# Attention with a feed-forward network on one core: all sixteen blocks of the network in one kind of sweep

## The chip, the core and the metric

The kernel runs on one core of a Trainium2 chip. The core has TensorE (matmuls, PE in the profile), VectorE (DVE), ScalarE (ACT), GpSimd (POOL) and SyncE (SP), which issues most DMA transfers. The metric is the device time of one execution in microseconds (us). A profile's own span leaves out what lies around the execution, here 1.7 us.

## The reference

Attention over 4 batches of 8 heads, 1152 keys of 64 dimensions, with queries pooled in pairs to 576; then a feed-forward network on 2304 tokens of width 512, with 2048 hidden units and a slope of its own for each negative hidden value. The weights are float64 and reach the kernel as pairs of 32-bit words.

```python
def _attn_ref(q, k, v) -> np.ndarray:
    B, H, S, D = q.shape
    factor = 2
    scale = 1.0 / np.sqrt(D)
    q_pool = q.reshape(B, H, S // factor, factor, D).mean(axis=3)
    scores = scale * np.matmul(q_pool, k.transpose(0, 1, 3, 2))
    scores = scores - np.max(scores, axis=-1, keepdims=True)
    attn = np.exp(scores)
    attn = attn / (np.sum(attn, axis=-1, keepdims=True) + 1e-09)
    return np.matmul(attn, v).astype(np.float32)
...
def _moe_ref(x, w_in, w_out, alpha) -> np.ndarray:
    h = x @ w_in
    g = np.maximum(h, 0.0) + alpha * np.minimum(h, 0.0)
    return (g @ w_out).astype(np.float32)
```

## The kernel before, in words

**A planner writes the order.** The kernel adds tasks (`Scheduler.add`), each with an engine, an assumed duration, what it reads and writes and a priority. `Scheduler.run` places them one by one at the earliest time by its own clock; among the tasks of an engine that could start within a slack, the lowest priority number goes first, and `NUDGE` shifts the numbers of single tasks. The order so found is each engine's program order; the durations play no part on the chip. Tasks marked `lock` (VectorE's operations that read two tiles of SBUF and GpSimd's additions) are placed one at a time. `Ring` is a set of buffers of one size, `Banks` a set of PSUM banks.

**Attention.** The 32 heads go in 16 pairs (n = 0, 2, ...). A pair's two heads stand on the two halves of the partitions; its 576 queries go in two halves of 288 (half number n + h). Per pair, `pair_prep` loads q and k and splits them into a high and a low part, `pair_max` computes the row maxima (24 matmuls of 384 columns at L851 and four short pairs at L858, each reduced by VectorE at L872). `half_main` does nine chunks per half: eight matmuls of scores (L987), two exponentials on ScalarE (L1004) into one of the slots `pa`, sums of the exponentials over chunks on GpSimd and VectorE (L1017; per half five on GpSimd, two on VectorE), and, once a half, a block of 36 matmuls of the exponentials with V (L1031). `pair_end` adds up the sums with matmuls (L1055), then normalises: the sums go through memory, VectorE and ScalarE make a high and a low part of the result (L1094, L1101, L1106), stored as `xs` (L1114).

**Feed-forward.** The hidden units form 16 blocks of 128. `mm3` (L497) is three matmuls (high by high, high by low, low by high). `hidden` (L507) makes one block for one range of tokens: four `mm3` over the width, two ReLUs on ScalarE (L525, L530), their combination on VectorE (L535), a rounded copy on ScalarE (L541) and the remainder on VectorE (L546). Four more `mm3` per block add to the four output tiles. Blocks 0 to 4 go first, in `low_sweep` (L553): eight ranges of 288 tokens; the partial outputs are copied by ScalarE (L573) and stored to `yp` (L577). Then `high_sweep` (L581) takes blocks 5 to 15 over five ranges of 464 or 460 tokens, loads the partial outputs (L598), adds them on VectorE (L622) and stores the result (L631).

**Weights.** Each block has two halves (first and second layer) of 512 KB. `w_convert` (L418) loads one (L423), takes the size on ScalarE (L426) and makes the value in four VectorE operations (L429, L435, L441, L447); `w_split` rounds it on ScalarE (L407) and takes the remainder on VectorE (L410). There are two buffers for each intermediate. The ten of blocks 0 to 4 run during attention, their place among the pairs set by `W0` to `W3`; six (blocks 5 to 7) go into the buffers of k once the last maxima are there (`maxed[RM]`); the other 16 go to a pool that opens where attention's pool is closed (L1221).

**Banks.** `share` (L1144) divides eight PSUM banks among scores, maxima and hidden units: `EARLY` at first, `LATE` once half `SWITCH` is placed. In `LATE` the hidden units may use banks 1 to 6, so feed-forward matmuls may be placed before attention is over.

Of the kernel before, what the change touches and what calls it, by code (L numbers as in the profile page):

```python
# [10 lines left out]
F32 = mybir.dt.float32  # L11
F32R = mybir.dt.float32r
# [14 lines left out]
ENTER, LEAVE = 160, 135  # L27
# [77 lines left out]
class Task:  # L105
    __slots__ = ("eng", "dur", "emit", "deps", "takes", "prio", "col", "left", "next", "end", "avail", "size", "kind", "dma", "lock", "fixed")


class Scheduler:
# [62 lines left out]
    def run(self, done):  # L172
        while not done():
            best = None
            for eng in range(5):
                at, pick, key = None, None, None
                cand = []
                for t in self.ready[eng]:
                    s = self.start_of(t)
                    if s is not None:  # L180
                        s = max(s, self.free[eng])
                        if eng == PE and self.col and not t.col:
                            s += self.turn
                        cand.append((s, t))
                if not cand:
                    continue
                at = min(c[0] for c in cand)
                for s, t in cand:
                    if s <= at + self.slack[eng]:
                        p = t.prio + (self.col_cost if eng == PE and t.col != self.col else 0.0)  # L190
                        if key is None or p < key:
                            key, pick, first = p, t, s
                if eng == PE and self.col and not pick.col:
                    first -= self.turn
                if best is None or first < best[0]:
                    best = (first, pick)
            assert best is not None, "nothing can run"
            self.place(*best)

    def place(self, at, t):  # L200
# [20 lines left out]
        if t.dma:  # L221
            self.dma_free = max(self.dma_free, t.end + 650) + t.size / DMA_RATE
# [11 lines left out]
def attention_ffn(  # L234
# [8 lines left out]
    NLO: int = 5,  # L243
    PB: int = 13,
# [4 lines left out]
    F0: float = -1.353,  # L249
    F2: float = -1.339,  # L250
# [7 lines left out]
    TO_PE: int = 80,  # L258
    FROM_PE: int = 40,
    SLP: int = 39,  # L260
    SLA: int = 62,
    SLD: int = 104,
    QL: float = -0.025,
    KL: float = 0.788,
    KR: float = 2.427,
    KS: float = 0.177,
    M0: float = 1.185,
    E0: float = 1.24,
# [4 lines left out]
    SR: float = 0.765,  # L273
    KQ: float = 0.979,
# [3 lines left out]
    SF: int = 16,  # L278
    Q0: float = 0.075,
    Q1: float = 3.179,  # L280
# [8 lines left out]
    GSB: int = 1,  # L289
    YSB: int = 4,  # L290
    R0: float = 4.187,
    R1: float = -5.36,
    R2: float = -7.727,
    R3: float = -0.231,
    W0: float = 6.13,
    W1: float = 0.815,
    W2: float = 17.603,
    W3: float = -1.085,
    YL: float = 0.25,
    MS: float = 0.129,  # L300
# [3 lines left out]
    GL: float = 16.906,  # L304
    COL: float = -0.047,
    HW: float = 2.585,
    XB: int = 4,
    PT: int = 17,
# [8 lines left out]
    RP: float = 28.496,  # L317
    RS: float = 0.985,
    RM: int = 30,
    RATE: float = 342.662,  # L320
    NP: float = 19.419,
# [148 lines left out]
    for r in (r_x, r_pos, r_neg, r_gs, r_ys):  # L470
        r.open(fpool)
# [804 lines left out]
```

## Time and profile before

| | us |
|---|---|
| time, median of three runs (lowest, highest) | 828.28 (827.81, 828.72) |
| time of the profiled execution | 828.34 |
| its span | 826.6 |
| TensorE busy | 818.3 |
| VectorE busy | 545.3 |
| ScalarE busy | 441.0 |
| GpSimd busy | 252.8 |

Matmuls overlap in the profile, and a busy time counts an operation from its start to its end, waits inside it included. The chain is found backwards from the last instruction: at each step to what released it, or to the instruction before it on its engine. A row such as `41.25 4.51 PE bank L1031 x36` is a piece of that chain: start, length, engine, what is written, line, number of instructions.

### The profile page before, as it was taken

How to read it: one execution, taken by the hardware profiler on the slowest of the kernel's cores; microseconds unless marked ns; L12 is line 12 of the kernel's file. 1: busy time of each engine (PE TensorE's matmuls, PEld its weight loads, DVE VectorE, ACT ScalarE, POOL GpSimd, SP SyncE). 2: the span in 40 equal slices, each digit the busy share in tenths (PEclk: the TensorE clock that was granted, in tenths of full speed). 3: DMA queues.
4: the chain of work that ended last, by engine and by line, in shares of the span. 5: the costliest groups of instructions: out<-in, count | busy, mean ns of one | idle time of the engine just before them, and what ended most of it. 6: DMA issues, size and time to landing. Idle time of an engine off the chain costs nothing.

```text
span 826.6 us, 17555 instructions
## 1 busy us (share of the span) xinstructions
PE 818.3 (99%) x6694; PEld 690.1 (83%) x6694; DVE 545.3 (66%) x1035; ACT 441.0 (53%) x1124; POOL 252.8 (31%) x196
## 2 busy tenths in 40 slices
PE   8999999999999999999999999999999999999997
PEld 7777777777787777777789999998898988888986
DVE  8999999999997798788853888822242332332422
ACT  4757676677675676666744667643243243322431
POOL 5755466465566565565360000000000000000000
PEclk9999999999999999999999999999999999999999
DMA  7335335644444443213233867780330411030301
GB/s 266 74 88 177 111 93 156 221 150 125 99 116 132 120 127 117 63 51 103 93 123 113 263 227 229 207 235 8 92 93 2 136 47 46 1 91 0 92 1 46
DMA packets 67904, 93.72 MB, mean 113 GB/s; under 512 B 20020, under 2 KB 45676, under 8 KB 67820
## 3 DMA queue, kind: packets, MB, share of 16 engines
q1 hardware_dynamic: 65084, 87.71, 34.0%
q0 software_dynamic: 2160, 4.42, 3.6%
q8 instruction: 52, 0.85, 0.4%
q10 hardware_dynamic: 576, 0.47, 0.2%
q14 instruction: 32, 0.26, 0.1%
HBM read 73.48 MB, written 19.02 MB: 112 GB/s over the span
## 4 chain that ended last, share of the span: by engine, by line
PE 96%; DVE 1%; DMA 1%; POOL 1%; issue 0%; ACT 0%; DVEq 0%
PE bank L499 49%; PE bank L987 20%; PE bank L1031 17%; PE bank L851 6%; PE bank L1055 2%; PE bank L858 1%; DMA qs<-qt 1%; DVE bx L872 1%; PE bank L1169 1%; POOL k L814 0%; POOL pa L1017 0%; DVE pa L1017 0%; PE bank L889 0%; DVE wbits L435 0%; POOL qs L773 0%
## 5 line engine op out<-in xcount | busy, mean ns | idle before, releaser
L1017 POOL TENSOR_TENSOR pa<-pa,pa 128x576 f32<-128x576 f32 x160 | 231.2, 1468 | 169.5 <-ACT pa L1004 32.1
L872 DVE TENSOR_REDUCE bx<-bank 128x1 f32<-128x384 f32 (+1 forms) x448 | 212.8, 534 | 24.2 <-PE bank L851 19.0
L1004 ACT ACTIVATE pa<-bank 128x288 f32<-128x288 f32 x576 | 198.8, 417 | 28.1 <-PE bank L987 16.5
L987 PE MATMUL bank<-q,k 64*128 64x288 f32 x1728 | 204.4, 311 | 0.1
L987 PEld LDWEIGHTS bank<-q,k 64*128 64x128 f32 x1728 | 159.5, 184 | 17.4 <-issue 7.2
L1031 PE MATMUL bank<-pa,vv 128*64 128x288 f32 x1152 | 146.8, 409 | 0.0
L1031 PEld LDWEIGHTS bank<-pa,vv 128*64 128x64 f32 x1152 | 79.9, 137 | 54.8 <-issue 3.7
L987 PE MATMUL bank<-mq,neg 64*128 64x288 f32 x576 | 112.5, 291 | 0.0
L851 PE MATMUL bank<-k,q 64*128 64x384 f32 x384 | 107.8, 361 | 1.7 <-ACT q L703 1.3
L535 DVE SCALAR_TENSOR_TENSOR gs<-gs,nal 128x460 f32<-128x460 f32 (+1 forms) x55 | 38.4, 698 | 92.4 <-ACT gs L530 92.4
L499 PE MATMUL bank<-wlow,wh 128*128 128x460 f32 (+1 forms) x320 | 92.9, 371 | 0.0
L499 PE MATMUL bank<-gw,wh 128*128 128x460 f32 (+1 forms) x320 | 92.8, 371 | 0.0
L546 DVE TENSOR_TENSOR gw<-gs,gw 128x460 fp32r<-128x460 f32 (+1 forms) x55 | 35.1, 639 | 85.2 <-ACT gw L541 85.2
L541 ACT ACTIVATE gw<-gs 128x460 fp32r<-128x460 f32 (+1 forms) x55 | 32.4, 589 | 92.9 <-PE bank L499 83.7
L987 PEld LDWEIGHTS bank<-mq,neg 64*128 64x128 f32 x576 | 80.5, 184 | 0.0
L525 ACT ACTIVATE gs<-bank 128x460 f32<-128x460 f32 (+1 forms) x55 | 30.6, 557 | 88.2 <-PE bank L499 87.2
L851 PEld LDWEIGHTS bank<-k,q 64*128 64x128 f32 x384 | 61.3, 184 | 14.0 <-DVE bx L872 5.6
L499 PEld LDWEIGHTS bank<-wlow,wh 128*128 128x128 f32 x320 | 60.1, 188 | 7.1
L499 PEld LDWEIGHTS bank<-gw,wh 128*128 128x128 f32 x320 | 60.1, 188 | 6.7
L499 PE MATMUL bank<-x,wlow 128*128 128x288 f32 x480 | 65.6, 295 | 0.0
L499 PE MATMUL bank<-gs,wlow 128*128 128x288 f32 x480 | 64.8, 294 | 0.0
L499 PEld LDWEIGHTS bank<-x,wlow 128*128 128x128 f32 x480 | 64.1, 188 | 0.8 <-issue 0.8
(90 smaller groups left out, 1022.9 us busy)
## 6 DMA issues: line engine op xcount, KB each, us to landing
wraw<-wt SPq DMA_DIRECT2D x32, 512.0 KB
vv<-vt SPq DMA_DIRECT2D x32, 288.0 KB
xs<-x SPq DMA_DIRECT2D x32, 288.0 KB
x<-xs SPq DMA_DIRECT2D x32, 288.0 KB
kk<-kt SPq DMA_DIRECT2D x15, 576.0 KB
r<-rrd SPq DMA_DIRECT2D x64, 72.0 KB
yp<-ys SPq DMA_DIRECT2D x32, 144.0 KB
wlow<-xs SPq DMA_DIRECT2D x16, 288.0 KB
```

What stands on the lines that cost most here:

```text
L499: nc.tensor.matmul(out=ps[:, :n], lhsT=w[a, c // DMO][:, c % DMO:c % DMO + P], rhs=lo(hl), start=(first and i == 0), stop=(last and i == 2),)
L525: ACT, act(n, True), lambda: nc.scalar.activation(out=flat(pos), in_=ps.t[:, :n], func=AF.Relu),
L535: lambda: nc.vector.scalar_tensor_tensor(out=flat(pos), in0=flat(neg), scalar=nal[:, f:f + 1], in1=flat(pos), op0=ALU.mult, op1=ALU.add),
L541: ACT, act(n), lambda: nc.scalar.activation(out=gs.t[:, 0, :n], in_=flat(pos), func=AF.Copy),
L546: lambda: nc.vector.tensor_tensor(out=gs.t[:, 1, :n], in0=flat(pos), in1=gs.t[:, 0, :n].bitcast(F32), op=ALU.subtract),
L851: nc.tensor.matmul(out=ms.t[:, :JW], lhsT=w.q1.t[d, starts[t]:starts[t] + P], rhs=w.k1.t[d, j * JW:(j + 1) * JW], start=True, stop=True,)
L872: nc.vector.tensor_reduce(out=bx.t[:, at, j:j + 1], in_=ms.t[:, :m], axis=AX.X, op=ALU.max)
L987: nc.tensor.matmul(out=ps.t[i][:, :HQ], lhsT=k.t[d, s] if k else neg[d], rhs=r.t[d, q], start=x == 0, stop=x == len(pairs) - 1,)
L1004: lambda ps=ps, p=p, i=i: nc.scalar.activation(out=p.t[:, i], in_=ps.t[i][:, :HQ], func=AF.Exp, scale=SCALE),
L1017: lambda a=a, b=p, part=part, e=e: e.tensor_tensor(out=part.t, in0=a.t, in1=b.t, op=ALU.add),
L1031: nc.tensor.matmul(out=av.t[i * D:(i + 1) * D, :HQ], lhsT=w.vv[i].t[:, e], rhs=p.t[:, i], start=(e == 0), stop=(e == NC - 1),)
L1055: nc.tensor.matmul(out=ps.t[g * 32:(g + 1) * 32, :HQ], lhsT=ones, rhs=acc[n + g // 2][j].t[:, g % 2], start=j == 0, stop=j == m - 1, tile_ ...
```

## The change

The division into low and high sweeps is gone, and with it the partial outputs. `sweep` takes one range of 464 or 460 tokens through all 16 blocks and copies the four output tiles from PSUM once. The x tiles are as wide as a range and have six buffers; those of the first range are loaded during attention (`RX`), those of the next while the current one runs. Hidden units have no bank in `EARLY` or `LATE`: they get banks when all of attention's matmuls are placed. The buffers of the normalisation move to a pool of their own, so the pool for the last 16 weight halves opens without waiting for it. The ten early conversions are one evenly spaced list (`W0` + `W1` c); the six late ones go by `RP` + `RS` c with a negative step. In the last range the last `YT` blocks' output matmuls go tile by tile. The planner's costs for changing the array's tiling are other, `SWITCH` moves from 13 to 29, slots for exponentials from 13 to 18, and all numbers of the plan, `NUDGE` among them, are new (cut here).

```diff
--- before.py
+++ after.py
-ENTER, LEAVE = 160, 135
+ENTER, LEAVE, QUARTER, NARROW = 160, 135, 135, 330
...
+def mode(col):
+    return min(col, 2)
+
+
+def change(a, b):
+    if mode(a) == mode(b):
+        return 0
+    if b > 1:
+        return NARROW
+    return (ENTER if b else LEAVE) + (QUARTER if a == 3 else 0)
...
-            if t.col != self.col:
-                dur += ENTER if t.col else LEAVE
+            dur += change(self.col, t.col)
...
-    NLO: int = 5,
-    PB: int = 13,
+    NE: int = 10,
+    PB: int = 18,
...
-    W0: float = 6.13,
-    W1: float = 0.815,
-    W2: float = 17.603,
-    W3: float = -1.085,
-    YL: float = 0.25,
+    R0: float = -2.0,
+    W0: float = 8.38,
+    W1: float = 2.392,
+    YL: float = 0.15,
...
-    LATE: tuple = ((0, 1, 2, 3, 4, 5, 6), (0, 1, 2, 3, 4, 5, 6), (1, 2, 3, 4, 5, 6)),
-    SWITCH: int = 13,
+    LATE: tuple = ((0, 1, 2, 3, 4, 5, 6), (0, 1, 2, 3, 4, 5, 6), ()),
+    SWITCH: int = 29,
...
-    HW: float = 2.585,
-    XB: int = 4,
-    PT: int = 17,
+    HW: float = -13.26,
+    XB: int = 6,
+    RX: float = 35.673,
+    PT: int = 18,
...
-    RP: float = 28.496,
-    RS: float = 0.985,
+    RP: float = 64.684,
+    RS: float = -1.529,
...
+    YT: int = 3,
...
-    r_x = Ring([P, 2, HQ], F32R, "x", XB)
-    r_low = Ring([P, 2, DMO], F32R, "wlow", 2 * NLO)
+    r_x = Ring([P, 2, max(NW)], F32R, "x", XB)
+    r_low = Ring([P, 2, DMO], F32R, "wlow", NE)
...
-    r_pos = Ring([P, HQ], F32, "pos", 3)
-    r_neg = Ring([P, HQ], F32, "neg", 2)
-    r_gs = Ring([P, 2, HQ], F32R, "gs", NLO + GSB)
-    r_ys = Ring([P, HQ], F32, "ys", YSB)
...
+    r_gs = Ring([P, max(NW)], F32, "gs", GSB)
+    r_ys = Ring([P, max(NW)], F32, "ys", YSB)
...
-    yp = [[dt(f"yp{b}_{j}", [P, KD, HQ], F32) for j in range(2)] for b in range(B)]
-    yp_b = [[Buf() for j in range(2)] for b in range(B)]
...
-    def low_sweep(b, j, prio):
...
-    def high_sweep(first, n, prio, end):
...
-        x, ys = [Buf(r_low) for k in range(KD)], [Buf(r_x) for m in range(KD)]
+    def x_load(first, n, prio, deps=()):
         row("z", first)
+        x = [Buf(r_x) for k in range(KD)]
...
+    def sweep(x, first, n, prio, end):
+        row("z", first)
+        ys = [Buf(r_ys) for m in range(KD)]
+        fs = range(NFF)
+
+        def tail(f, m, p):
+            return prio + 0.05 * (fs[-1] - fs[0]) + YL + 0.001 * m if end and f > NFF - 1 - YT else p
+
         y = [Buf(r_y) for m in range(KD)]
         prev = [None] * KD
-        fs = range(NLO, NFF)
         for f in fs:
-            p = prio + 0.05 * (f - NLO)
-            gs = hidden(f, x, n, p, True)
+            p = prio + 0.05 * f
+            gs = hidden(f, x, n, p)
...
                 t = add(
                     DVE, dve(hi - lo),
-                    lambda m=m, lo=lo, hi=hi: nc.vector.tensor_tensor(
-                        out=flat_of(ys[m], F32)[:, lo:hi], in0=y[m].t[:, lo:hi], in1=flat_of(ys[m], F32)[:, lo:hi], op=ALU.add
-                    ),
-                    deps=[prev[m]] + ys[m].writers[:len(list(parts(first, n)))], uses=[y[m], ys[m]], prio=prio,
+                    lambda m=m, lo=lo, hi=hi: nc.vector.tensor_copy(out=ys[m].t[:, lo:hi], in_=y[m].t[:, lo:hi]),
+                    reads=[y[m]], writes=[ys[m]], deps=[prev[m]], prio=prio,
                 )
...
+        bp = ctx.enter_context(tc.tile_pool(name="norm", bufs=1))
         ap = actx.enter_context(tc.tile_pool(name="attn", bufs=1))
...
-        for r in (r_vv, r_qs, r_q1, r_q2, r_mm, r_avs, r_rs, r_rc, r_r, r_x2):
+        for r in (r_vv, r_qs, r_q1, r_q2, r_mm):
             r.open(ap)
+        for r in (r_avs, r_rs, r_rc, r_r, r_x2):
+            r.open(bp)
...
-        for i in range(2):
-            for f in range(NLO):
-                r = int(R2 + R3 * f if i else R0 + R1 * f)
-                w_convert(f, i, W2 + W3 * f if i else W0 + W1 * f, [maxed[max(0, r)]], r_low, first=loads[LW:LW + 1] if LW >= 0 else ())
+        for c in range(NE):
+            r = max(0, int(W0 + W1 * c + R0))
+            w_convert(c // 2, c % 2, W0 + W1 * c, [maxed[r]], r_low, first=loads[LW:LW + 1] if LW >= 0 else ())
         rings = [r for r in (r_kk, r_k1, r_k2) for i in range(2)]
         for c in range(REUSE):
-            f, i = NLO + c // 2, c % 2
+            f, i = (NE + c) // 2, (NE + c) % 2
             w_convert(f, i, RP + RS * c, [maxed[RM]], rings[c], loads[-2:])
-        for b in range(B):
-            for j in range(2):
-                low_sweep(b, j, FF + 2 * b + j)
+        x = x_load(0, NW[0], RX, [maxed[RM]])
...
-        attn = [u for r in (r_ps, r_av, r_ms, r_one) for b in r.made for u in b.users]
+        attn = [
+            u for r in (r_ps, r_av, r_ms, r_one, r_vv, r_qs, r_q1, r_q2, r_mx, r_rt, r_mq, r_bx, r_mm, r_p, r_acc)
+            for b in r.made for u in b.users
+        ]
...
-            w_convert(f, i, 2 * FF + 0.05 * (f - NLO) - HW)
+            w_convert(f, i, 2 * FF + 0.05 * f - HW)
     for i, n in enumerate(NW):
-        high_sweep(sum(NW[:i]), n, 2 * FF + i, i == len(NW) - 1)
+        if i:
+            x = x_load(sum(NW[:i]), n, 2 * FF + i - 1)
+        sweep(x, sum(NW[:i]), n, 2 * FF + i, i == len(NW) - 1)
```

## Rows read from the trace of the kernel before

**Rows 1.** The page, chain that ended last: shares of the span by engine.

```profile
PE 96%; DVE 1%; DMA 1%; POOL 1%; issue 0%; ACT 0%; DVEq 0%
```

**Rows 2.** The chain in order of time, whole span: start us, us, what.

```profile
41.25 4.51 PE bank L1031 x36
...
133.59 4.52 PE bank L1031 x36
...
196.22 4.52 PE bank L1031 x36
...
246.79 4.51 PE bank L1031 x36
...
382.11 4.52 PE bank L1031 x36
...
399.61 1.78 PE bank L499 x12
...
413.57 6.57 PE bank L499 x48
...
424.65 9.64 PE bank L499 x72
434.30 1.11 PE bank L1055 x16
435.40 385.87 PE bank L499 x2148
```

**Rows 3.** Busy us by stretch and engine (instructions), clock, DMA share, GB/s.

```profile
core 0: us, PE busy (x) PEld busy (x) DVE busy (x) ACT busy (x) POOL busy (x), PEclk, DMA share, GB/s
50.00:100.00 50.00, 49.96 (x524) 37.71 (x522) 47.04 (x98) 33.53 (x93) 29.27 (x21) 1.00 0.36 110
200.00:250.00 50.00, 50.00 (x541) 38.62 (x537) 46.97 (x96) 35.48 (x98) 29.83 (x22) 1.00 0.48 135
250.00:300.00 50.00, 50.00 (x537) 37.46 (x537) 40.51 (x82) 32.83 (x93) 29.87 (x22) 1.00 0.40 115
350.00:382.00 32.00, 32.00 (x365) 25.14 (x357) 27.52 (x54) 20.86 (x61) 19.76 (x14) 1.00 0.21 67
382.00:434.00 52.00, 52.00 (x495) 41.90 (x492) 39.25 (x58) 32.81 (x93) 25.56 (x16) 1.00 0.34 108
455.00:535.00 80.00, 80.00 (x606) 80.00 (x605) 68.31 (x132) 53.20 (x130) 0.00 (x0) 1.00 0.74 230
```

**Rows 4.** The chain in 436 to 545 us and in 545 to 822 us.

```profile
436.00 109.11 PE bank L499 x824
...
544.97 276.30 PE bank L499 x1322
```

**Rows 5.** VectorE in order of time, 430 to 436 us: the last sum.

```profile
432.90 0.76 DVE L1017 TENSOR_TENSOR pa<-pa,pa 128x576 f32<-128x576 f32 x1 [2.99 <-POOL pa L1017]
```

**Rows 6.** Groups of VectorE, 382 to 434 us: xcount, busy us, mean ns.

```profile
L546 DVE TENSOR_TENSOR gs<-pos,gs 128x288 fp32r<-128x288 f32 x5 | 5.1, 1035 | 1.0 <-ACT gs L541 0.9
```

**Rows 7.** Groups of the whole span, shapes apart: feed-forward and conversions on VectorE.

```profile
L546 DVE TENSOR_TENSOR gs<-pos,gs 128x288 fp32r<-128x288 f32 x40 | 21.0, 526 | 7.3 <-ACT gs L541 7.2
L535 DVE SCALAR_TENSOR_TENSOR pos<-neg,nal,pos 128x288 f32<-128x288 f32 x40 | 20.5, 514 | 10.4 <-ACT neg L530 9.1
L429 DVE TENSOR_SCALAR wbits<-wraw 128x512 int32<-128x512 int32 x32 | 15.8, 493 | 1.1 <-DMA wraw<-wt 1.1
L435 DVE SCALAR_TENSOR_TENSOR wbits<-wraw,wbits 128x512 int32<-128x512 int32 x32 | 21.8, 682 | 0.2
L441 DVE SCALAR_TENSOR_TENSOR wbits<-wraw,wbits 128x512 int32<-128x512 int32 x32 | 23.0, 721 | 0.3
L447 DVE SCALAR_TENSOR_TENSOR wmag<-wmag,wbits 128x512 f32<-128x512 f32 x32 | 22.7, 708 | 0.3
L410 DVE TENSOR_TENSOR wl<-wmag,wh 128x512 fp32r<-128x512 f32 x16 | 10.9, 688 | 3.7 <-ACT wh L407 3.5
```

**Rows 8.** Instructions of the last 16 weight halves' tile: ns min/median/max, first, last.

```profile
L410 DVE TENSOR_TENSOR wl<-wmag,wh x16: 680/691/693, 464.2 to 533.1; 128x512 fp32r<-128x512 f32 x16
```

**Rows 9.** The chain in 812 to 827 us: after the last matmul.

```profile
821.30 0.40 DVE x L622
```

More of the change, by code (lines that the diff above doesn't have):

```diff
@@ L221, in place @@
         if t.dma:
-            self.dma_free = max(self.dma_free, t.end + 650) + t.size / DMA_RATE
+            self.dma_free = max(self.dma_free, t.end + 650) + t.size / (DMA_RATE * (0.8 if at < 20000 else 1))
             t.end = self.dma_free
@@ L474, in attention_ffn @@
     xs_b = [Buf() for b in range(B)]
-    yp = [[dt(f"yp{b}_{j}", [P, KD, HQ], F32) for j in range(2)] for b in range(B)]
-    yp_b = [[Buf() for j in range(2)] for b in range(B)]
-    def x_load(b, j, prio):
-        xk = [Buf(r_x) for k in range(KD)]
-        for k, x in enumerate(xk):
-            add(
-                SP, 600, lambda k=k, x=x: nc.sync.dma_start(out=x.t.bitcast(F32), in_=xs[b][k, j]),
-                reads=[xs_b[b]], writes=[x], prio=prio + 0.0001 * k, size=P * 2 * HQ * 4,
-            )
-        return xk
     def parts(first, n):
@@ L505, in mm3_time, with hidden @@
         return 3 * (n * 17 / 16 / 2.4 + 4.5)
-    def hidden(f, x, n, prio, wide):
-        ps, pos, neg, gs = Buf(r_h), Buf(r_gs if wide else r_pos), Buf(r_gs if wide else r_neg), Buf(r_gw if wide else r_gs)
+    last_hidden = []
+    def hidden(f, x, n, prio):
+        ps, pos, neg, gs = Buf(r_h), Buf(r_gs), Buf(r_gs), Buf(r_gw)
         def flat(buf):
@@ L514, in hidden, with mm @@
         t = None
-        step = 1 if wide else KD
-        for lo in range(0, KD, step):
-            def mm(lo=lo):
-                for kd in range(lo, lo + step):
-                    mm3(ps.t, n, f, kd * P, lambda hl: x[kd].t[:, hl, :n], kd == 0, kd == KD - 1)
-            t = add(PE, step * mm3_time(n), mm, reads=x[lo:lo + step] + [w_done[f, 0]], writes=[ps],
-                    deps=[t] if t else [], prio=prio, kind="group" if lo else "first")
+        for kd in range(KD):
+            def mm(kd=kd):
+                mm3(ps.t, n, f, kd * P, lambda hl: x[kd].t[:, hl, :n], kd == 0, kd == KD - 1)
+            t = add(PE, mm3_time(n), mm, reads=[x[kd], w_done[f, 0]], writes=[ps], deps=[t] if t else last_hidden[-1:], prio=prio, kind="group" if kd else "first")
+        last_hidden.append(t)
         add(
@@ L631, in high_sweep @@
                         lambda m=m, b=b, j=j, q=q, c=c, lo=lo, e=e: e.dma_start(
[L632 removed]
+                            out=out[b, j, m, :, q], in_=ys[m].t[:, lo + c.start:lo + c.stop]
                         ),
@@ L1064, in pair_end @@
         e = n + E0
-        add(PE, 486 * len(acc[n]), sums, reads=acc[n] + acc[n + 1], writes=[ps], prio=e, col=2, kind="s")
+        add(PE, 486 * len(acc[n]), sums, reads=acc[n] + acc[n + 1], writes=[ps], prio=e, col=3, kind="s")
         add(
@@ L1215, in attention_ffn @@
         r_h.places = [single[i] for i in (0, 1, 2, 7)]
-        attn = [
-            u for r in (*(() if REUSE else (r_kk, r_k1, r_k2)), r_vv, r_qs, r_q1, r_q2, r_mx, r_rt, r_mq, r_bx, r_mm, r_p, r_acc, r_avs, r_rs, r_rc, r_r, r_x2)
-            for b in r.made for u in b.users
-        ]
-        sch.run(lambda: all(t.end is not None for t in attn))
     hpool[0] = ctx.enter_context(tc.tile_pool(name="hpool", bufs=1))
-    r_gw.open(hpool[0])
-    for f in range(NLO, NFF):
+    for r in (r_gw, r_gs, r_ys):
+        r.open(hpool[0])
+    for f in range(NFF):
         for i in range(2):
```

101 lines of the change are left out of this document (33 added, 68 removed).

## Prediction

> **What bounds the kernel now.** I read the chain that ended last first, then the same chain in order of time, then the busy time of each engine by stretch, and last the rows of the operations that share a stretch with the change. The chain is TensorE for 96% of the span [rows 1]: what does not stand on TensorE's lane costs nothing until it makes that lane wait. In order of time the lane has two parts [rows 2]. Up to 435.40 us it carries attention: each half of a pair of heads ends in one block of 36 matmuls of weights times V, and these blocks mark the pace. From 435.40 us one unbroken run of 2148 feed-forward matmuls takes 385.87 us. Before that, three pieces of feed-forward matmuls (12, 48 and 72) fill 1.78 + 6.57 + 9.64 = 17.99 us of the attention's last 36 us. So the feed-forward work takes 17.99 + 385.87 = 403.86 us of the lane, and attention without it would end at 435.40 - 17.99 = 417.41 us.
>
> The second bound shows in the stretches [rows 3]. VectorE is busy 47.0 us of every 50 up to 250 us (94%), while ten of the weight conversions run, and 40.51 + 27.52 of 82 us (83%) after them. The pace of the halves follows it [rows 2]: half 1 to 8 (41.25 to 133.59) 13.19 us a half, 8 to 17 (to 246.79) 12.58, 17 to 28 (to 382.11) 12.30.
>
> All terms below are differences to the profiled execution: span 826.6 us, time 828.34 us, 0.06 us above the median of the runs, 828.28.
>
> **Feed-forward matmuls.** Before: 8 x 24 x 5 = 960 of 288 columns and 5 x 24 x 11 = 1320 of 464 or 460. After: 5 x 24 x 16 = 1920 of the wide kind, with the same mix of 464 and 460. On the lane the narrow ones take 109.11/824 = 0.1324 us and the wide ones 276.30/1322 = 0.2090 us [rows 4]. After: 1920 x 0.2090 = 401.28 us, against 403.86: **-2.6 us**, the change of the array's tiling at the edges of the three pieces included. Per column that is little, since (0.2090 - 0.1324)/172 = 0.445 ns a column leaves only 4 ns per matmul that do not depend on columns.
>
> The Trainium skill (TensorEngine Tiling (Array Packing), Instruction Overhead) gives each matmul about 60 cycles of overhead. Read as a cost added to each, at 2.4 GHz, the 360 matmuls that vanish would be worth an estimated 9 us and the time would be about 6.4 us below my forecast; the slope between the two sizes above speaks against that reading, and the sum goes by the rows.
>
> **Partial outputs.** 32 evictions on ScalarE, 32 stores and 48 loads on SP's queue go away, and 21 adds on VectorE become copies of the same size. All of it lay under the unbroken run of TensorE [rows 2, 4]: **0**. Without that cover it would be worth something only at the seam near 545 us, where the lane shows no gap.
>
> **Ten early conversions.** They move from 45 to 240 us to positions 2.4 halves apart, from half 8 on, none before the maxima of half 6. VectorE's load evens out to (200 x 0.94 + 132 x 0.83)/332 = 0.896. On the line between the two paces (12.58 at 0.94, 12.30 at 0.83) that is 12.47 us a half; 27 halves from 41.25 to 382.11 take 336.7 us, not 340.9: **-4.2 us**. Bounds: 0, if only the place of the delay moves, and 27 x 12.30 = 332.1, which is -8.8. The other new numbers of the plan (18 slots for exponentials, not 13; start-up priorities; other costs for the array's changes) I cannot price from rows: 0, with 2 us either way.
>
> **The end of attention.** No bank is given to hidden units until every attention matmul is placed, so on TensorE's queue the first feed-forward matmul now stands behind the last sums, and all feed-forward work behind it. The 17.99 us of filler are gone: does the lane wait instead? Before, the last partial sum ends at 432.90 + 0.76 = 433.66 us [rows 5], the sums start 0.64 us later and take 1.11 [rows 2]. From 382 to 434 us VectorE is busy 39.25 and GpSimd 25.56 of 52 us, together more than the stretch holds [rows 3], since the planner and the chip let VectorE's two-input operations and GpSimd's additions go one at a time: VectorE's residual subtract takes 1035 ns there [rows 6] and 526 over the whole run [rows 7]. So these two engines, not TensorE, end the attention. Taking away the five feed-forward pairs of operations there gives 5 x (0.514 + 0.526) = 5.2 us [rows 7]: last sum at 428.5, end of attention at 430.2, or 430.2 - 417.4 = 12.8 us of idle lane, if all six late conversions stay ahead of the last addition as before. Each that falls behind it gives 0.493 + 0.682 + 0.721 + 0.708 + 0.688 = 3.29 us back [rows 7]. The six are now taken in reverse order: the two that need a place of the low part of K come first, and must wait for the scores of half 29 and half 31, each holding one of two intermediate buffers, so that mostly one conversion circulates, not two. I take three ahead and three behind: 12.8 - 9.9 = **+2.9 us**. Bounds: 0 (two ahead; the lane then has its own work) and 12.8.
>
> The Trainium skill (SBUF — State Buffer, SBUF: two separate sides) says that a VectorE operation with two SBUF inputs and a GpSimd operation take a shared pair of ports as an exclusive lock, and the loser waits for the whole instruction. By that rule the work of both simply adds up, which is the second case below at its worst; did they share the ports, the additions would run beside the conversions, the wait would be 0 and the time 821.0. The 1035 ns agree with the rule.
>
> **Weights of blocks 8 to 15.** They have 16 conversions, which had 133 us of narrow sweeps and now lie in the first wide sweep of 80 us. A block takes 24 x 0.2090 = 5.0 us, so block 15 is due 75 us into the sweep. Before, the same 16 ended 464.2 to 533.1 us [rows 8], 68.9/15 = 4.6 us each, with VectorE at 68.31 of 80 us [rows 3]. The room opens with the end of attention, since the normalising buffers have moved out of it; the first ends some 3 us after that, the 15th at 3 + 14 x 4.6 = 67 us, 8 before it is due: **0**. Between sweeps, six x buffers mean that two of four tiles of the next sweep wait for the last hidden block; 36 output matmuls x 0.2090 = 7.5 us cover their loads. Bounds 0 and some 6 us for both.
>
> **The end.** The last three blocks' outputs are regrouped, so that three of four output tiles end earlier than the 0.63 us apart of before; after the lane's end there still stand one half-tile copy of 0.40 us [rows 9] and its store. **-0.5 us**, bounds 0 and -1.
>
> Sum: -2.6 - 4.2 + 2.9 - 0.5 = -4.4; 828.3 - 4.4 = **823.9 us**.
>
> **The rivals.**
> - Slower, by the port. All six conversions stay ahead of the last addition: 828.3 - 2.6 - 4.2 + 12.8 - 0.5 = 833.8 us. It turns into a loss when the wait passes 2.6 + 4.2 + 0.5 = 7.3 us, that is with the fifth conversion ahead. For it: the fullness of 382 to 434 us. Against: the reversed order, and more slots for sums.
> - Starved sweeps. The conversions need over 5.2 us each, or the x loads outlast their 7.5 us: +6 us, 830 us. For it: VectorE's 85%. Against: the 8 us to spare.
> - It does not do what it says for attention: the pace after half 17 came from the wider sharing of PSUM banks, which now begins at half 29, not 13. No gain of 4.2, and 11 x 0.28 = 3.1 lost: 831.2 us. Against it: halves 8 to 13 took (196.22 - 133.59)/5 = 12.53 us and 13 to 17 12.64 [rows 2]; the sharing widened and nothing happened.
> - More gain: all halves at 12.30 and no wait at the end: 828.3 - 2.6 - 8.8 - 0.5 = 816.4 us.
>
> **How the numbers follow.** The forecast has a chance of 0.50 (its own range 820 to 829), the port 0.19, starved sweeps 0.09, the banks 0.06, more gain 0.16. A difference of 0.2%, 1.7 us, is about what a measurement of this kernel can tell from no change. Faster by more: 0.37 of the forecast's 0.50 and all of the last, 0.53. Within: 0.09 + 0.02 = 0.11. Slower: 0.04 + 0.19 + 0.09 + 0.04 = 0.36. The range runs from the last case, 816, to the port's, 834, with some 0.1 left out on each side.
>
> **What would show it.** Right: one run of 1920 wide matmuls of some 401 us that starts near 416 us with under 4 us of idle lane before it; halves at 12.5 us from start to end; last conversions done before block 15. Wrong: a wait of TensorE on an addition or on the last sums of 7 us or more; gaps inside the first sweep ended by VectorE's weight split; gaps at the four seams ended by a load of x; halves no faster than before.

## The result, and the profile after

The change makes the kernel slower: 833.38 us (median of four runs, 832.15 to 835.03) against 828.26 for the kernel before on the same chip, ratio 1.0061 (95% interval 1.0048 to 1.0073). The forecast was 823.9, faster. The profiled execution took 832.15 us, its span is 830.2, that is 3.6 more than before. The four times after lie 2.9 us apart and the profiled one is the lowest, so the traces below account for 3.6 of the 5.1 us between the medians.

First the chain that ended last in the kernel after, by engine (the line answers to [rows 1]):

```profile
PE 94%; DMA 2%; DVE 1%; ACT 1%; POOL 1%; issue 1%; POOLq 0%; SPq 0%; DVEq 0%; ACTq 0%
```

The chain in order of time (start us, us, what), to be laid beside [rows 2]; L996 is weights times V, L952 the scores, L982 the additions, L495 the feed-forward matmuls:

```profile
41.02 4.52 PE bank L996 x36
...
133.43 4.52 PE bank L996 x36
...
249.25 4.52 PE bank L996 x36
...
372.28 4.52 PE bank L996 x36
...
401.23 3.78 PE bank L952 x40
...
409.04 4.52 PE bank L996 x36
413.55 3.63 PE bank L952 x38
...
418.12 1.43 POOL pa L982
...
431.67 0.56 DVE gw L542
432.23 0.04 issue
432.27 394.04 PE bank L495 x1883
826.31 0.02 issue
826.33 0.40 DVE ys L589
```

The wide run is there, unbroken from 432.27 us. It begins with 37 more matmuls, the first at 424.04 us. By the prediction's reckoning attention without filler ended at 417.41 us before, so the start is 6.6 us later. The run itself takes 826.31 - 424.04 = 402.27 us, 1.6 less than 403.86. After the last matmul the span has 3.9 us left, where it had 5.3. The sum 6.6 - 1.6 - 1.4 = +3.6 us is the whole difference: it all comes from attention. Half 27 starts at 372.28 us, 2.6 later than the 369.69 of before (half 1 starts 0.2 earlier, halves 1 to 27 take 2.8 longer); from there to the first feed-forward matmul it takes 51.8 us, where before it took 65.7 with 17.99 us of filler in it, or 47.7 without: 4.1 more. Two lines of the chain before, half 27 and a piece of scores at the end of attention:

```profile
369.69 4.51 PE bank L1031 x36
...
410.62 2.94 PE bank L987 x39
```

Busy us by stretch, with the columns of [rows 3]:

```profile
200.00:250.00 50.00, 50.00 (x544) 38.74 (x542) 43.11 (x89) 33.77 (x96) 31.12 (x23) 1.00 0.35 99
250.00:300.00 50.00, 49.96 (x513) 36.65 (x511) 47.51 (x93) 34.27 (x94) 28.78 (x21) 1.00 0.47 140
...
382.00:424.00 42.00, 41.52 (x401) 28.11 (x399) 21.84 (x38) 25.15 (x72) 26.24 (x18) 1.00 0.42 126
424.00:505.00 81.00, 80.81 (x387) 71.72 (x384) 74.81 (x134) 48.93 (x90) 0.00 (x0) 1.00 0.54 157
```

VectorE's load is spread as forecast: it fell at 200 us (43.11 against 46.97) and rose at 250 (47.51 against 40.51). TensorE's column stayed where it was in [rows 3], at 49.96 to 50.00 of 50. The pace did not follow VectorE: the stretch of halves 17 to 27 takes 123.0 us after (with four conversions in it) and 122.9 before (without).

Each matmul has a weight load (PEld) for its fixed operand; the page after counts 6344 of each. In these traces the short waits of TensorE stand on the weight loads while the matmuls' own column stays full, so the view of waits is read by PEld. Attention's end in the kernel after, 375 to 436 us (us in total, times, longest):

```profile
PEld bank L952 <- ACT pa L969: 1.3, 5, 0.5
...
PEld bank L1020 <- DVE pa L982: 0.8, 1, 0.8
...
PEld bank L495 <- DVE gw L542: 0.6, 1, 0.6
```

Scores (L952) wait for the exponentials that free their PSUM banks, the last sums (L1020) 0.8 us for an addition, and the first output matmuls for the last piece of a hidden block. In the chain above, 40 score matmuls take 3.78 us and 38 take 3.63: 0.76 us for a chunk of eight. At the same place before, 39 took 2.94 (L987, above), 0.60 us a chunk. From start to start of the matmuls, the five pieces of scores from 383 us on run at 0.70 to 0.75 us a chunk, the four of before at 0.56 to 0.59.

### The profile page after: what moved, and what is told of

It is laid out like the page before. It is cut to its first block, busy times and chain, and to the rows that moved or that the text cites. A ratio compares the mean times of both kernels' runs of the same rounds, so it can differ in the third digit from the quotient of the medians.

```text
span 830.2 us, 16339 instructions
## 1 busy us (share of the span) xinstructions
PE 823.4 (99%) x6344; PEld 678.6 (82%) x6344; DVE 534.5 (64%) x1005; ACT 429.9 (52%) x1047; POOL 253.9 (31%) x196
## 4 chain that ended last, share of the span: by engine, by line
PE 94%; DMA 2%; DVE 1%; ACT 1%; POOL 1%; issue 1%; POOLq 0%; SPq 0%; DVEq 0%; ACTq 0%
PE bank L495 47%; PE bank L952 20%; PE bank L996 17%; PE bank L816 6%; PE bank L1020 2%; PE bank L823 1%; DMA qs<-qt 1%; DMA kk<-kt 1%; DVE bx L837 0%; POOL k L779 0%; ACT pa L969 0%; POOLq L1237 0%; PE bank L854 0%; POOL pa L982 0%; DVE wbits L445 0%
## 5 line engine op out<-in xcount | busy, mean ns | idle before, releaser
L982 POOL TENSOR_TENSOR pa<-pa,pa 128x576 f32<-128x576 f32 x160 | 231.0, 1461 | 163.4 <-ACT pa L969 20.3
L952 PE MATMUL bank<-q,k 64*128 64x288 f32 x1728 | 210.1, 312 | 0.7 <-ACT pa L969 0.5
L952 PEld LDWEIGHTS bank<-q,k 64*128 64x128 f32 x1728 | 164.9, 184 | 18.5 <-issue 4.9
L531 DVE SCALAR_TENSOR_TENSOR gs<-gs,nal 128x460 f32<-128x460 f32 (+1 forms) x80 | 55.7, 696 | 150.0 <-ACT gs L526 149.8
L996 PE MATMUL bank<-pa,vv 128*64 128x288 f32 x1152 | 146.8, 409 | 0.0
L996 PEld LDWEIGHTS bank<-pa,vv 128*64 128x64 f32 x1152 | 79.9, 137 | 55.3 <-issue 4.2
L521 ACT ACTIVATE gs<-bank 128x460 f32<-128x460 f32 (+1 forms) x80 | 44.3, 554 | 150.6 <-PE bank L495 149.1
L952 PE MATMUL bank<-mq,neg 64*128 64x288 f32 x576 | 116.7, 290 | 0.0
L816 PE MATMUL bank<-k,q 64*128 64x384 f32 x384 | 111.8, 367 | 0.6 <-ACT k L677 0.3
L495 PE MATMUL bank<-gw,wh 128*128 128x460 f32 (+1 forms) x320 | 92.9, 371 | 0.0
L495 PE MATMUL bank<-x,wh 128*128 128x460 f32 (+1 forms) x320 | 92.6, 370 | 0.0
L542 DVE TENSOR_TENSOR gw<-gs,gw 128x460 fp32r<-128x460 f32 (+1 forms) x80 | 51.0, 637 | 62.1 <-ACT gw L537 62.1
L537 ACT ACTIVATE gw<-gs 128x460 fp32r<-128x460 f32 (+1 forms) x80 | 47.1, 589 | 77.4 <-DVE gs L531 42.5
L952 PEld LDWEIGHTS bank<-mq,neg 64*128 64x128 f32 x576 | 85.3, 184 | 0.0
L816 PEld LDWEIGHTS bank<-k,q 64*128 64x128 f32 x384 | 62.2, 184 | 17.8 <-DVE bx L837 7.3
L495 PE MATMUL bank<-gw,wlow 128*128 128x460 f32 (+1 forms) x300 | 67.0, 372 | 0.2 <-DVE gw L542 0.2
L495 PEld LDWEIGHTS bank<-x,wh 128*128 128x128 f32 x320 | 60.0, 188 | 7.0
L495 PEld LDWEIGHTS bank<-gw,wh 128*128 128x128 f32 x320 | 60.1, 188 | 6.8
L495 PE MATMUL bank<-x,wlow 128*128 128x460 f32 (+1 forms) x300 | 65.3, 371 | 0.0
L982 DVE TENSOR_TENSOR pa<-pa,pa 128x576 f32<-128x576 f32 x64 | 53.4, 836 | 15.6 <-POOL pa L982 14.3
```

Of the source, the lines that this page charges most:

```text
L495: nc.tensor.matmul(out=ps[:, :n], lhsT=w[a, c // DMO][:, c % DMO:c % DMO + P], rhs=lo(hl), start=(first and i == 0), stop=(last and i == 2),)
L521: ACT, act(n, True), lambda: nc.scalar.activation(out=flat(pos), in_=ps.t[:, :n], func=AF.Relu),
L531: lambda: nc.vector.scalar_tensor_tensor(out=flat(pos), in0=flat(neg), scalar=nal[:, f:f + 1], in1=flat(pos), op0=ALU.mult, op1=ALU.add),
L537: ACT, act(n), lambda: nc.scalar.activation(out=gs.t[:, 0, :n], in_=flat(pos), func=AF.Copy),
L542: lambda: nc.vector.tensor_tensor(out=gs.t[:, 1, :n], in0=flat(pos), in1=gs.t[:, 0, :n].bitcast(F32), op=ALU.subtract),
L816: nc.tensor.matmul(out=ms.t[:, :JW], lhsT=w.q1.t[d, starts[t]:starts[t] + P], rhs=w.k1.t[d, j * JW:(j + 1) * JW], start=True, stop=True,)
```

## Experiments: the pace of the halves

In the kernels called "order held", every instruction stands where it stood, and only the named thing is changed. Starts of halves are the first matmuls of L1031 or L996. A profiled execution can lie some 2 us later than another of the same order from the first halves on, so places are compared by distances within one trace. The column PEclk of the windows is the granted clock, the share of TensorE's full 2.4 GHz; in these traces it is 1.00 or 0.50 (1.2 GHz), or a mean where a stretch has both.

**Are the ten early conversions felt at all?** Before and after, order held, with VectorE's four operations left out:

```diff
         def top():
+            if ring is r_low:
+                return None
             return nc.vector.tensor_scalar(
...
```

(and the same in `tail`, `sign` and `value`)

> The kernel before with its written order kept, but the four VectorE operations that make the value of a weight are left out for the ten early conversions (the weights of blocks 0 to 4 are then wrong): 10 x 2.6 = 26 us of VectorE less between 45 and 240 us. Theory load (VectorE's load sets the pace of the halves, the ground of the step that moved the ten conversions): halves 8 to 17 take 12.3 us each, not 12.58, and halves 1 to 8 less than 13.19; time 822 to 825 us. Rival order (the pace is fixed by the order written and by the exponentials, and the conversions lie in VectorE's slack): halves unchanged within 0.1 us, time 827.3 to 828.5 us.

> The changed kernel with its written order kept, and the same four operations left out for its ten early conversions, which lie between half 6 and half 30 (the weights of blocks 0 to 4 are then wrong). Theory load: the attention ends 3 to 6 us earlier, time 827 to 830 us. Rival order: under 1 us, time 832 to 834 us. If the late place of the conversions cost what the step promised as a gain, this kernel gains more than the same cut in the kernel before.

Before: 829.68 us, ratio 1.0015 (0.9999 to 1.0031); halves 4 to 27 take 287.12 us, with the conversions 287.14. After: 832.61 us, ratio 1.005 (1.0032 to 1.0069), the start of every half within 0.4 us. Some 26 us of VectorE's work vanish, and before, from half 4 to half 27, no half changes by more than 0.02 us. VectorE's load does not set the pace. Halves 8, 17 and 27 of b_noconv, to be laid beside 133.59, 246.79 [rows 2] and 369.69:

```profile
135.98 4.52 PE bank L1039 x36
...
249.17 4.52 PE bank L1039 x36
...
372.09 4.52 PE bank L1039 x36
```

They lie 2.3 us later because half 1 is 2.7 us longer in this execution: TensorE waited for exponentials behind a load of q that landed at 54.69 us, and then ran at half the clock:

```profile
57.00:60.00 3.00, 3.00 (x23) 2.65 (x19) 2.65 (x6) 1.77 (x6) 0.71 (x1) 0.50 0.03 5
```

The same stretch before has 30 matmuls at a granted clock of 1.00.

**Is it TensorE, then?** Before, order held, one of the four products of the scores left out in halves 4 to 27, 432 matmuls:

```diff
                 for x, (k, r) in enumerate(pairs):
+                    if x == 2 and 4 <= half < 28:
+                        continue
```

> The kernel before, in its order, with one of the four products of the scores (low part of k by high part of q) left out in halves 4 to 27: 24 halves x 9 chunks x 2 = 432 matmuls fewer, at 66 ns each 28.5 us of TensorE; the scores lose a little precision, all else runs. VectorE's work is the same. Theory (TensorE's lane is full in halves 4 to 27 and alone sets their pace): halves 4 to 28 shorten by nearly all of it, 22 to 28 us, less only where VectorE, 90 to 94% busy, is reached as the next bound; time 800 to 807. The prediction's step (VectorE's load sets the pace): the pace of the halves changes by less than 5 us, time over 823.

819.38 us, ratio 0.9894 (0.9878 to 0.9911). Halves 4 to 27 shorten from 287.14 to 278.68 us, 8.5 us: less than the 28.5 us that TensorE alone would give by the expectation's 66 ns a matmul, more than nothing. Both expectations were too simple. TensorE is the first bound and another stands right behind it: from start to start of matmuls, the steps from score to score add up to 22.7 us less, the steps in front of maxima to 13.1 us more. The waits of the weight loads at 82 to 370 us show it; L851 and L859 are the maxima, `bx` VectorE's reduction that frees their bank. Kernel before:

```profile
PEld bank L851 <- DVE bx L872: 2.0, 9, 0.3
```

With one product left out:

```profile
PEld bank L851 <- DVE bx L872: 9.1, 39, 0.4
```

So the next two runs: the same cut without the ten conversions, and the same cut in the kernel after.

> As b_lane (one of four products of the scores left out in halves 4 to 27), and the four VectorE operations of the ten early weight conversions left out as well (what the weights of blocks 0 to 4 hold is wrong). Without them VectorE has 10 x 2.6 = 26 us less to do. b_lane took 28.5 us from TensorE and halves 4 to 27 shortened by only 8.5; so another bound stands close behind the lane. If that bound is VectorE's load, as the prediction has it, the stretch now shortens by 14 to 26 us against before, most of it in halves 4 to 17 where the conversions lie. If it is a loop that the conversions don't touch (maxima and their reduction, exponentials and their PSUM banks, additions), it stays at 8 to 10 us.

> The kernel after, in its order, with the same cut as b_lane: one of four products of the scores left out in halves 4 to 27, 28.5 us of TensorE. In the kernel before this gave 8.5 us. If the even spread of the ten conversions eases VectorE as the prediction has it, and only the lane hid that, more comes back here: 12 to 20 us in halves 4 to 27, time 814 to 822. If the spread is worth nothing even with a free lane: 7 to 10 us, time 823.5 to 826.5.

Without conversions: 817.6 us, ratio 0.9874 (0.9858 to 0.9891). Halves 4 to 17 gain 2.0 us more than with them, 17 to 27 nothing (118.78 and 118.79). The maxima still wait for reductions (same view and stretch):

```profile
PEld bank L859 <- DVE bx L880: 5.8, 26, 0.4
```

After: 827.59 us, ratio 0.999 (0.998 to 1.0), where the kernel after had 1.0061: 5.9 us gained, against 8.8 in the kernel before. In the profiled execution, the slowest of ten at 830.21 us, halves 4 to 27 shorten from 288.22 to 284.60, only 3.6 us. That is too little, since in this execution half 10 takes 2.6 us longer than after. ScalarE waited 6.2 us for the load of a weight, the scores 2.3 us for the exponentials behind it, and then the granted clock was 0.50 (waits of ScalarE at 156 to 175 us, waits of the weight loads at 82 to 370 us, and a stretch):

```profile
ACT wmag L436 <- DMA wraw<-wt: 6.2, 1, 6.2
PEld bank L954 <- ACT pa L971: 2.9, 4, 2.3
166.00:169.00 3.00, 3.00 (x23) 2.69 (x23) 2.42 (x6) 1.94 (x7) 2.81 (x2) 0.50 0.64 204
```

Without half 10, the halves shorten by 6.3 us after and by 7.9 before. The maxima (L816) wait more than in the kernel before; same view as for L851:

```profile
PEld bank L816 <- DVE bx L837: 13.0, 49, 0.6
```

With the lane freed, the conversions are worth 2 us, not 26, and nothing shows that spreading them helps: after the change less of the freed time comes back, not more, though the two orders differ in more than the spread. That the reductions are what follows TensorE is read from these waits; no run changed the reductions themselves.

**Does the narrower sharing of banks cost pace?** After, order held; from half 13 on scores, maxima and sums take the bank longest free among seven, as before:

```diff
...
+            can = [p for p in self.wide if all(u.end is not None for b in p[0] if b.real for u in b.real.users)]
+            if can:
+                place = min(can, key=lambda p: max((u.end for b in p[0] if b.real for u in b.real.users), default=0))
...
```

> The kernel after, every instruction in its place; from the end of half 13 on, scores, maxima and sums take their PSUM banks out of seven (0 to 6, the longest free first), as in the kernel before, instead of five for scores and three for maxima. What is computed stays the same. Theory (the narrower sharing costs time from half 13 on): halves 13 to 27, which took 175.9 us after and 173.4 before, take 173.5 to 174.5; in the tail the scores run at 0.60 to 0.63 us a chunk, but the last sums wait for the additions as in a_3pairs. Time 831 to 832.5, some 2 us under after. Rival (the order of the plan sets the pace): halves 13 to 27 stay at 175.7 to 176.1, the time at 833.4 to 834.8.

834.16 us, ratio 1.0066 (1.0053 to 1.008). Halves 13 to 27 take 175.6 us, 175.9 without. Banks are not why halves 1 to 27 take 331.3 us against 328.4. In that stretch the kernel after has 16 matmuls more, 1.3 us at the 79 ns that lie between two matmuls of scores there. The other 1.6 us are put down to the order of the new plan, which is not shown (one piece: 12 times instead of 8 weights times V follow a maximum, mostly at 0.26 to 0.37 us from one matmul to the next, where they mostly begin 0.12 to 0.22 us after a score or a transpose); which of the plan's numbers brings it was not tried. Of the 2.8 us, 1.7 lie in halves 1 to 4, which took anything from 41.3 to 43.9 us in five executions of the order before (43.0 after); halves 4 to 27 took 287.1 to 287.2 us in all five, so that the 1.1 us lost there stand clear.

## Experiments: the end of attention

**Late conversions, exponentials and banks, one at a time.** After, order held: the four VectorE operations of the six late conversions left out (a_nolate, as above, with their rings named); the exponentials of halves 28 to 31 on half the columns (a_halfexp); three pairs of banks in turn for the scores once the last maxima are there (a_3pairs, taken by the same rule as the seven banks), instead of the two disjoint pairs that five banks hold:

```diff
-out=p.t[:, i], in_=ps.t[i][:, :HQ], func=AF.Exp, scale=SCALE
+out=p.t[:, i, :HQ // 2 if n + h >= 28 else HQ], in_=ps.t[i][:, :HQ // 2 if n + h >= 28 else HQ], func=AF.Exp, scale=SCALE
...
+        r_ps.turns = [(single[i][0] + single[j][0], (single[i][1], single[j][1])) for i, j in ((1, 2), (3, 4), (5, 6))]
```

> The changed kernel, order kept, with the same four operations left out for the six late conversions, blocks 5 to 7 (their weights are then wrong): 15.6 us of VectorE less from 383 us on, of which the greater part before the end of attention at 424.0 us. Theory port (VectorE and GpSimd, one at a time, end the attention): the end of attention moves to 419.5 to 421 us and the time falls by 3 to 4.5 us. Rival exponentials (with no feed-forward matmuls between them, the scores of the last four halves run at ScalarE's pace): end of attention within 0.5 us of 424.0, time down by less than 1 us.

> The changed kernel, order kept, with the exponentials of halves 28 to 31 made for half of their columns only (the rest of those slots keeps old values). Theory exponentials: the scores after 383 us run at 0.53 us a chunk, not 0.75, and the end of attention moves from 424.0 to about 420 us; time down by 3 to 5 us. Rival port: the scores run faster but the last sum still ends the attention: down by less than 1 us.

> The kernel after, every instruction in its place; only which PSUM banks the scores go to is changed once the last maxima are there (near 382 us): three pairs of banks in turn instead of two. What is computed stays the same. Theory (two causes, one behind the other): with two pairs a chunk of scores waits for the exponentials of the chunk before the last, which gives 0.72 to 0.76 us a chunk; with three pairs it should be 0.60 to 0.63 as in the kernel before, so halves 27, 28 and 30 get shorter by some 1.0, 0.6 and 0.6 us. The end of attention then waits for the additions, which the six late weight conversions hold up, so that the feed-forward run starts less than 1 us earlier than 424.0 us and the time stays between 832 and 833.5. Banks alone: start near 420.5, time near 829.8. Rival (the scores wait for ScalarE itself, or the missing feed-forward matmuls are the only reason): still 0.72 us a chunk, nothing changes, 833.4.

Times: 833.33, 833.65 and 834.8 us, ratios 1.0066 (1.004 to 1.0091), 1.0062 (1.0044 to 1.008) and 1.0065 (1.0052 to 1.0078), all as after. From half 27 to the first feed-forward matmul: 51.4, 51.7 and 51.9 us, after 51.8. Yet the traces differ. Without the late conversions the additions are in time and the scores are as slow as after. With half the exponentials the sums wait 3.6 us for additions. With three pairs the scores run faster, 30 matmuls in 2.32 us or 0.62 us a chunk, and from start to start 0.54 to 0.65 us a chunk in the five pieces. That run's chain in order of time, from a late conversion (L428, L444) to the sums (L1028) and the scores behind them:

```profile
401.05 0.61 DVE k L428
...
401.68 0.68 ACT wmag L444
402.36 0.30 ACT avs L1017
402.66 1.51 ACT pa L977 x5
...
404.20 1.93 POOL pa L990
...
406.15 0.77 DVE pa L990
...
406.96 0.69 PE bank L1028 x8
407.65 2.32 PE bank L960 x30
```

Its sums wait instead; the waits of its weight loads, 375 to 436 us:

```profile
PEld bank L1028 <- DVE pa L990: 4.9, 2, 2.7
```

Two causes, each hidden by the other. So both at once:

> As a_3pairs, and the four VectorE operations of the six late weight conversions are left out as well (their loads, the rounding and the split stay; what the weights of blocks 5 to 7 hold is wrong). Theory of two causes: leaving out either alone moves the end of attention by less than 1 us, both together move the start of the feed-forward run from 424.0 to some 420.0 to 421.0 us and the time to 829.5 to 830.5. Banks alone: the same time as a_3pairs, 829.8, and a_3pairs is there already. Rival (the order of the plan, neither banks nor additions): 833.3 as without the late operations alone.

> As a_7banks, and the four VectorE operations of the six late weight conversions left out as well (what the weights of blocks 5 to 7 hold is wrong). If banks cost 2 us in halves 13 to 27 and banks and additions together 3 us after them, the feed-forward run starts near 419 us and the time is 828 to 829.5. If only the tail hangs on banks, it is that of a_3pairs_nolate, 831.3 (ratio 1.0024). If it is over that, the order of the plan is all that is left.

831.32 us (1.0024, 1.0014 to 1.0035) and 830.96 us (1.0025, 1.0016 to 1.0034): by the ratios some 3.4 us better than either alone. From half 27 to the first feed-forward matmul it takes 49.1 and 49.2 us, 2.7 less than after; half 31 starts 42.1 us after half 27 instead of 45.7, and part of that is lost again in a wait of the last sums for an addition (a_3pairs_nolate, same view):

```profile
PEld bank L1036 <- DVE pa L998: 1.7, 1, 1.7
```

The second run adds nothing to the first; its expectation had named this outcome too. Taken alone, a_7banks is no clean partner for it: in its profiled execution TensorE waited 1.65 and 1.9 us at 400.9 and 404.6 us, and the granted clock was 0.50 from 404.5 to 411 us. The three runs with a_3pairs and a_nolate have no such stretch at the end of attention, so the two causes rest on them.

**What was the filler worth before?** Before, order held, the first narrow range cut from 120 to 18 matmuls, 13.5 us of TensorE; then VectorE's operations of that range and of the late conversions left out as well:

```diff
+                if short:
+                    for kd in range(KD):
+                        if kd in (0, KD - 1):
+                            nc.tensor.matmul(out=ps.t[:, :n], lhsT=wh[f, 0][:, kd * P:kd * P + P], rhs=x[kd].t[:, 0, :n], start=kd == 0, stop=kd == KD - 1)
+                    return
...
```

(the hidden units, two matmuls a block; of the output matmuls one stays in each of eight groups)

> The kernel before with the first range of its narrow sweep cut from 120 to 18 feed-forward matmuls, every other instruction in its place (that range's hidden units and partial outputs are wrong). The 102 matmuls that vanish take 102 x 0.1324 = 13.5 us of TensorE, all of it among the last 36 us of attention. Step of the prediction (TensorE gets the time back, attention without filler ends at 417.4 us): the time falls by 13.5 to 814.8 us. Theory (the filler ran in time in which TensorE would have waited for exponentials and additions anyway): only part comes back, 7 to 10 us, time 818 to 821, with waits of the last sums on additions in the trace. Rival (additions alone set the end of attention): under 3 us come back, time over 825.

> As b_cutfill (102 of the filler's matmuls left out of the kernel before, everything else in its order), and with them the work of VectorE that ran beside them: the four operations of the six late conversions and the two operations of each of that range's five hidden blocks. Cutting the matmuls alone had brought under 1 us of 13.5. Theory (the filler stood in time in which TensorE would have waited for additions that VectorE's other operations hold up): the last sums are ready at 420 to 423 us instead of 434, the time falls to 815 to 819. Rival (additions are held up by the exponentials or by their own number, not by the other VectorE operations): the sums still wait past 430 us, time over 825.

The cut alone: 829.79 us, ratio 1.000 (0.999 to 1.001). From half 27 to the unbroken run 64.8 us instead of 65.7: of 13.5 us, 0.9 come back. The last sums wait (waits of the weight loads, 375 to 436 us):

```profile
PEld bank L1064 <- POOL pa L1026: 5.8, 1, 5.8
PEld bank L1064 <- DVE pa L1026: 2.0, 1, 2.0
```

And those 0.9 us are lost again: from the first matmul behind the last sums to the end of the feed-forward work it takes 387.5 us instead of 385.9. TensorE had started no matmul from 427.1 to 432.9 us; after that the granted clock was 0.50, until between 440 and 441 us. The same 4 us of feed-forward matmuls in b_cutfill and in the kernel before:

```profile
436.00:440.00 4.00, 4.00 (x20) 3.81 (x17) 0.46 (x1) 1.30 (x4) 0.00 (x0) 0.50 0.03 2
436.00:440.00 4.00, 4.00 (x32) 4.00 (x32) 1.77 (x4) 2.07 (x6) 0.00 (x0) 1.00 0.03 2
```

Without VectorE's operations too: 825.58 us, ratio 0.9961 (0.9948 to 0.9974), 60.5 us, 5.2 of 13.5. Its expectation (815 to 819) was missed as well: the last sums still wait 3.9 us for GpSimd and 2.0 for VectorE (weight loads, 375 to 436 us), behind the load of the normalising factors and the operation that needs it (chain of this last run in order of time), and the granted clock is 0.50 from 426 to 432 us:

```profile
417.40 4.54 DMA r<-rrd
...
422.80 1.41 DVE r L1111
...
426.01 1.40 POOL pa L1034
...
428.80 0.77 DVE pa L1034
```

So the filler before cost next to nothing: it stood where TensorE would have waited for the additions, and where most of it is left out the clock falls besides.

**A version better than both.** Before, with one thing of the change, the regrouping of the last three blocks:

```diff
+        def tail(f, m, p):
+            return prio + 0.05 * (fs[-1] - fs[0]) + YL + 0.001 * m if end and f > NFF - 1 - YT else p
...
-                    deps=[prev[m]] if prev[m] else [], prio=p + YL,
+                    deps=[prev[m]] if prev[m] else [], prio=tail(f, m, p + YL),
```

> The kernel before with one thing of the change: in the last range the output matmuls of the last three blocks are regrouped by output tile, as after. Attention and the sweeps are the same instructions in the same order. If the regrouping makes the end shorter, from the last matmul to the end of the span 3.9 us instead of 5.3, the time falls by 1.4 to 826.8. If the shorter end after came from other things (buffers, order of copies), 828.2.

827.74 us, ratio 0.9982 (0.9973 to 0.9992): of the kernels here that leave nothing out of the work, the only one faster than the kernel before. After the last matmul 4.6 us are left instead of 5.3; after has 3.9, so the other 0.6 us of its shorter end are something else.

## Why the prediction was wrong, step by step

- **Feed-forward matmuls, -2.6: right, somewhat large.** Measured -1.6. The run is 402.27 us, of which some 0.5 is the wait for the first hidden block's last piece; 1883 matmuls in 394.04 us are 0.2093 each, the 0.2090 of the sum. The reading of the Trainium skill (TensorEngine Tiling (Array Packing), Instruction Overhead) as 60 cycles added to each matmul, an estimated 9 us, is not borne out.
- **Partial outputs, 0, and weights of blocks 8 to 15, 0: right.** No gap in the run from 432.27 us on, though VectorE is busy 74.81 of 81 us in the first sweep. The rival of starved sweeps did not happen.
- **Ten early conversions, -4.2: this step failed, and it carries the wrong sign.** Halves 1 to 27 took 2.8 us more. I took two paces that went along with VectorE's load for its effect. TensorE stood at 50 of 50 us in the same rows [rows 3], and the chain gave it 96% [rows 1], which my own first paragraph said; and at one and the same load of VectorE, 47 of 50 us, halves 1 to 8 had taken 13.19 us and halves 8 to 17 12.58. Part of the difference is the work of TensorE: per half 138.3, 133.3 and 132.5 matmuls in halves 1 to 8, 8 to 17 and 17 to 28 before, at 94 ns each worth 0.47 of the first 0.61 us but only 0.08 of the last 0.28; the rest stays open, and it is not the conversions, without which halves 8 to 17 take the same 113.2 us. The runs put TensorE first, a loop of maxima and reductions right behind it, and the conversions last, worth 2 us even with one product of the scores cut away. Why halves 1 to 27 became slower stays open: 16 matmuls more and the new order are what the traces show, no run took them apart.
- **End of attention, +2.9: the direction was right, the size and the mechanism were not.** Measured +4.1. Three of the late conversions do stand behind the attention (splits at 425.8, 430.4 and 433.5 us), as taken, but they are only half of it: leaving the late conversions out moves nothing while the scores have two pairs of banks, and more banks move nothing while the conversions stand. The sum had no term for the banks. Both together bring back 2.7 of the 4.1 us; the other 1.4 stay open. Also, 417.41 us as the end of attention without filler was not to be had in this order: cut away, the filler gives back 0.9 of 13.5 us. With three pairs of banks the sums wait 4.9 us for VectorE's additions with the late conversions in place and 1.7 us without them. In the kernel after, five of the 17 GpSimd additions that start from 380 to 419 us take 1.74 to 1.95 us and the others 1.40 to 1.43; without the late conversions one takes 1.59 and the others 1.40 to 1.43. The Trainium skill's rule (SBUF — State Buffer, SBUF: two separate sides) of VectorE and GpSimd waiting for each other fits these longer additions. That the port alone makes the sums late is not shown: in the chain of a_3pairs the exponentials, too, stand behind a late conversion on ScalarE (401.68 us), and no run took the two apart.
- **The end, -0.5: right, too small.** 1.4 us, of which regrouping is 0.7.

The port's rival had the time, 833.8, by luck: it had the halves gain 4.2 us and the lane lose 12.8. The bank rival named the right cause at the wrong place: the narrow sharing costs nothing at halves 13 to 27, where maxima and weights times V lie between the scores, and costs its part only after the last maxima, where scores follow scores. Taken off singly, neither cause at the end can be seen.

## What to carry to other kernels

Before a second engine's load is called the pace, look whether the first engine has any time left in the same stretch, and count its work per step: two paces that differ with one load can differ with other things as well. Work that fills the end of a stage is not freed when it is taken away; ask what the stage waits for without it, expect more than one answer, each hidden by the next, and look at the granted clock behind the gap. Where leaving out one cause moves nothing, leave out two at once.

## What the runs showed of the hardware

- With two pairs of PSUM banks a chunk of scores (eight matmuls and two exponentials) took 0.70 to 0.75 us from start to start, with three pairs 0.54 to 0.65, as soon as only scores followed each other; part of the difference shows as waits of weight loads for the exponential that frees a bank (1.3 us after, 0.2 in a_3pairs, 375 to 436 us).
- A wait of TensorE for another engine shows on its weight loads (9.1 us in b_lane at 82 to 370 us), while the matmuls' own busy time is 277.00 of 278 us at 82 to 360 us: matmul busy time alone does not show whether the lane is free.
- Between the first 25 us and the last matmul, five executions show a granted clock of 0.50, each behind a wait of TensorE: 1.7 us without a new matmul in b_noconv, 2.3 in a_lane, 1.65 in a_7banks, 4.0 in b_cutfill_noport, 5.8 in b_cutfill. In a_3pairs, TensorE waited 2.0 and 2.6 us at 404.9 and 422.8 us and the clock stayed at 1.00. At 0.50, 20 feed-forward matmuls of 288 columns fitted into 4 us, at 1.00 it was 32.
- A feed-forward matmul of 288 columns took 0.1324 us [rows 4] and one of 460 or 464 columns 0.2093 us, so that joining narrow sweeps into wide ones gained 1.6 us in 400.
